# Attention kernel: exponentials three score banks wide instead of two, with a nine-slot ring for P

## The chip, the cores and the metric

The kernel runs on one core of one Trainium2 chip. The time is the device time of one execution in microseconds (us). Every version was run several times; the medians below are of its runs. The kernel before has a median of 1074.17 us in the 15 runs that stand beside the changed one (1072.96 to 1075.71).

A word on names. TensorE (PE in the profile) multiplies matrices, ScalarE (ACT) computes the exponentials, VectorE (DVE) copies and adds, GpSimd (POOL) helps. PSUM is the accumulator memory; the kernel's tile `ps` takes 8 banks of 128 x 512 fp32 in it.

## The reference, cut to what matters

```python
# x: 2048 x 512 bf16, 32 heads of width 16, feed-forward width 1792
qkv = layernorm(x) @ wqkv
scores = einsum("bhqd,bhkd->bhqk", q, k) * 16 ** -0.5      # 32 x 2048 x 2048
o = einsum("bhqk,bhkd->bhqd", softmax(scores), v)
h = x + o @ wo
out = h + relu(layernorm(h) @ w1 + b1) ** 2 @ w2 + b2
```

The scores are 134 million numbers, and each needs one exponential. That is what the kernel is built around.

## The kernel before

Heads are taken in 8 groups of 4, queries in 4 chunks of 512, keys in 16 tiles of 128. One *step* is one key tile for one group and one query chunk: 512 steps. In a step TensorE computes four 128 x 512 score tiles (QK, four matmuls packed into 32 rows each), ScalarE takes their exponential into P, and four packed matmuls multiply P by V (PV). One score tile of 512 columns is called a *unit* here; there are 2048.

```python
        def mk_qk(s):                                   # QK of step s: 4 units
            ...
                for j in range(4):
                    bnk = (4 * s + j) % 6               # score banks 0..5
                    ins = e.matmul(ps[:, bnk, :], lhsT=KT[32 * j:32 * j + 32, g, 128 * t:128 * (t + 1)],
                                   rhs=QT[32 * j:32 * j + 32, slot, :], ..., tile_position=(32 * j, 0))

        def mk_exp(s):                                  # two Exps of 1024 columns each
            for h2 in range(2):
                i = 2 * s + h2
                b0 = (4 * s + 2 * h2) % 6
                u0 = (2 * i) % 8                        # P ring of 8 slots
                n_exp[i] = N("act", 918, ... e.activation(out=PT[:, u0:u0 + 2, :],
                                     in_=ps[:, b0:b0 + 2, :], func=ACTF.Exp) ...,
                    deps=[n_qk[s], n_pv.get(s - 2)], ...)
```

`N(...)` does not issue anything. It hands a task to a list scheduler, which orders the tasks of each engine when the kernel is built, by priority and by its own estimates of when each could start. So a change of one task can move others.

First, everything that is neither score nor output (K and Q projections, V, output projection, feed-forward) goes through bank 7 alone. The evacuation of V alternates between two engines:

```python
            if t % 2 == 0:
                n_e = N("dve", 700, ...)     # VectorE
            else:
                n_e = N("act", 700, ...)     # ScalarE, between Exps
```

Second, where TensorE would idle, the scheduler puts in dummy matmuls by a zero matrix `zw`. They add zero to the output bank, so they are allowed only while an accumulation is open there, and at most six fit one gap:

```python
            if use_dum and e == "pe" and n.crit and self.oacc_open and t - self.free[e] > dum_min_gap:
                k = int((t - self.free[e] - 110.0) // dum_len)
```

Third, the softmax denominators. Each half chunk (four groups) ends with 1/Z, split into two bf16 parts of 16 rows, being spread over 128 partitions by two matmuls per group:

```python
        Rch = sb("Rch", [16, 512], BF16)     # Rcl and bsel likewise 16 rows
        ...
                    e.matmul(ps[:, b, :], lhsT=bsel[:, g4, :, :]..., rhs=Rch[:, :], start=True, stop=False)
                    return e.matmul(ps[:, b, :], lhsT=bsel[:, g4, :, :]..., rhs=Rcl[:, :], start=False, stop=True)
```

## Time and profile before

| what (profiled execution) | before |
|---|---|
| span | 1071.2 us |
| first Exp starts, last Exp ends | 44.6, 1011.2 us |
| busy: TensorE, ScalarE | 92%, 92% |
| mean granted TensorE clock | 0.987 |
| dummy matmuls | 1122 |

The prediction below shows the page and ScalarE's timeline. Two more lines belong here. The first is the page's row of the granted TensorE clock, one digit for each fortieth of the span (9 is 90% and more). The second, from the view of ScalarE's waits, says how long it stood before an Exp in all, how often, and the longest.

```profile
PEclk9996999899999999999999999999999999999999
```

```profile
ACT PT L724 <- PE ps L706: 26.6, 7, 22.1
```

The reader should see 26.6 us of standing, of which one wait is 22.1.

### The profile page before, as it was taken

How to read it: one execution, taken by the hardware profiler on the slowest of the kernel's cores; microseconds unless marked ns; L12 is line 12 of the kernel's file. 1: busy time of each engine (PE TensorE's matmuls, PEld its weight loads, DVE VectorE, ACT ScalarE, POOL GpSimd, SP SyncE). 2: the span in 40 equal slices, each digit the busy share in tenths (PEclk: the TensorE clock that was granted, in tenths of full speed). 3: DMA queues.
4: the chain of work that ended last, by engine and by line, in shares of the span. 5: the costliest groups of instructions: out<-in, count | busy, mean ns of one | idle time of the engine just before them, and what ended most of it. 6: DMA issues, size and time to landing. Idle time of an engine off the chain costs nothing.

```text
span 1071.2 us, 15193 instructions
## 1 busy us (share of the span) xinstructions
PE 980.2 (92%) x6461; PEld 267.0 (25%) x6461; DVE 318.3 (30%) x571; ACT 980.8 (92%) x1086; POOL 195.7 (18%) x312
## 2 busy tenths in 40 slices
PE   3886888999998999999998999999998999999998
PEld 1321222222222222222222222222222222222242
DVE  6504544411134322301145413210054324100151
ACT  6783999899999999999999999999999999999721
POOL 7203433100002411000012401000013400000021
PEclk9996999899999999999999999999999999999999
DMA  4500000000000000000000000000000000000000
GB/s 157 158 1 1 2 1 1 1 2 1 1 2 21 1 11 11 1 2 1 2 5 17 2 13 9 2 1 2 1 11 11 1 16 7 1 1 2 2 1 20
DMA packets 10466, 13.30 MB, mean 12 GB/s; under 512 B 925, under 2 KB 9374, under 8 KB 10398
## 3 DMA queue, kind: packets, MB, share of 16 engines
q1 hardware_dynamic: 8910, 9.71, 2.9%
q0 software_dynamic: 432, 1.57, 0.4%
q8 instruction: 51, 0.84, 0.3%
q10 hardware_dynamic: 1056, 1.05, 0.3%
q14 instruction: 17, 0.14, 0.0%
HBM read 9.97 MB, written 2.10 MB: 11 GB/s over the span
## 4 chain that ended last, share of the span: by engine, by line
ACT 82%; PE 14%; DVE 2%; DMA 1%; issue 1%; SPq 0%; POOL 0%; DVEq 0%
ACT PT L724 81%; PE ps L906 2%; PE ps L406 2%; PE ps L565 2%; PE ps L411 2%; PE ps L933 1%; PE ps L706 1%; DMA b1ld<-in_B_b_dram 1%; PE ps L741 1%; ACT xn L535 1%; PE ps L854 1%; DVE KT L588 1%; PE ps L595 1%; DVE kmx L599 1%; PE ps L660 1%
## 5 line engine op out<-in xcount | busy, mean ns | idle before, releaser
L724 ACT ACTIVATE PT<-ps 128x1024 bf16<-128x1024 f32 x1024 | 940.3, 1248 | 27.1 <-PE ps L706 26.6
L406 PE MATMUL ps<-KT,zw 128*128 128x512 bf16 x1122 | 341.9, 386 | 0.0
L741 PE MATMUL ps<-PT,Vp 128*32 128x512 bf16 x2048 | 205.4, 391 | 16.1 <-ACT PT L724 10.8
L706 PE MATMUL ps<-QT,KT 32*128 32x512 bf16 x2048 | 203.2, 387 | 15.6 <-ACT PT L724 4.5
L628 POOL TENSOR_TENSOR sq<-QT 128x512 bf16<-128x512 bf16 x32 | 33.3, 1039 | 438.8 <-DVE QT L625 424.4
L625 DVE TENSOR_SCALAR QT<-ps,cst 128x512 bf16<-128x512 f32 x32 | 24.0, 751 | 297.6 <-PE ps L565 297.6
L741 PEld LDWEIGHTS ps<-PT,Vp 128*32 128x32 bf16 x2048 | 52.7, 93 | 237.3 <-ACT PT L724 196.4
L706 PEld LDWEIGHTS ps<-QT,KT 32*128 32x128 bf16 x2048 | 51.6, 91 | 213.2 <-ACT PT L724 207.0
L406 PEld LDWEIGHTS ps<-KT,zw 128*128 128x128 bf16 x1122 | 64.9, 97 | 130.6 <-issue 129.6
L752 DVE COPY Osb<-ps 128x512 f32<-128x512 f32 x32 | 22.1, 690 | 141.7 <-PE ps L741 141.7
L924 POOL TENSOR_TENSOR h2T<-t 128x512 bf16<-128x512 bf16 x49 | 50.9, 1039 | 70.2 <-DVE t L921 70.2
L933 PE MATMUL ps<-wbig,h2T 128*128 128x512 bf16 x224 | 59.4, 382 | 1.1 <-issue 0.2
L906 PE MATMUL ps<-hnT,wbig 128*128 128x512 bf16 x224 | 55.6, 380 | 4.0 <-DVE t L921 3.2
L921 DVE TENSOR_SCALAR t<-ps,b1c 128x512 bf16<-128x512 f32 x49 | 36.8, 751 | 62.5 <-PE ps L906 62.5
L592 POOL TENSOR_TENSOR sq<-KT 128x512 bf16<-128x512 bf16 x28 | 29.3, 1047 | 72.8 <-PE ps L595 50.6
L565 PE MATMUL ps<-xnT,Wkp 128*128 128x512 bf16 x128 | 35.9, 407 | 5.3 <-DVE KT L588 2.2
L565 PE MATMUL ps<-xnT,Wqp 128*128 128x512 bf16 x128 | 34.0, 389 | 2.9 <-DVE kmx L599 0.8
L871 POOL TENSOR_SCALAR rstd<-mv 128x1 f32<-128x1 f32 x16 | 3.5, 219 | 165.0 <-DVE mv L869 164.8
L854 PE MATMUL ps<-wo,OT 128*128 128x512 bf16 x128 | 32.6, 381 | 0.9 <-DVE mv L869 0.6
L940 DVE TENSOR_TENSOR ost<-ps,hsb 128x512 bf16<-128x512 f32 x16 | 11.1, 692 | 73.4 <-PE ps L935 73.4
L648 DVE TENSOR_SCALAR qqs<-qqs,qst 128x512 f32<-128x512 f32 x32 | 17.5, 546 | 47.6 <-POOL qst L645 47.6
L588 DVE TENSOR_SCALAR KT<-ps,cst 128x512 bf16<-128x512 f32 x28 | 22.7, 809 | 27.8 <-PE ps L565 27.7
(98 smaller groups left out, 523.4 us busy)
## 6 DMA issues: line engine op xcount, KB each, us to landing
xin<-in_A_x_dram SPq DMA_DIRECT2D x16, 128.0 KB, 2.1
out_dram<-ost SPq DMA_DIRECT2D x16, 128.0 KB, 1.7
wbig<-in_B_w_dram SPq DMA_DIRECT2D x4, 448.0 KB
wbig<-in_B_w_dram SPq DMA_DIRECT2D x1, 1792.0 KB
wbig<-in_A_x_dram ACTq DMA_DIRECT2D x2, 512.0 KB, 9.2
wbig<-in_A_x_dram SPq DMA_DIRECT2D x2, 512.0 KB
h2T<-in_A_wqkv_dram POOLq DMA_DIRECT2D x2, 512.0 KB, 9.0
wv<-in_A_wqkv_dram POOLq DMA_DIRECT2D x1, 512.0 KB, 11.2
```

The source lines that it names most:

```text
L406: return e.matmul(ps[:, OB, :], lhsT=zw[:, :], rhs=KT[:, 0, 0:512], start=False, stop=False, skip_group_check=True)
L565: ins = e.matmul(ps[:, b, :], lhsT=W[:, dt, 4 * g:4 * g + 4, :].rearrange("p j r -> p (j r)"), rhs=xnT[:, dt, tok0:tok0 + 512], start=(dt ...
L588: n_e = N("dve", 660, (lambda g, kc: lambda e, b: e.tensor_scalar(out=KT[:, g, 512 * kc:512 * (kc + 1)], in0=ps[:, b, :], scalar1=cst[:, 1 ...
L628: n_s = N("pool", 1050, lambda e, b: e.tensor_tensor(out=sq[:, sslot, :], in0=QT[:, slot, :], in1=QT[:, slot, :], op=ALU.mult), deps=[n_e, ...
L706: ins = e.matmul(ps[:, bnk, :], lhsT=KT[32 * j:32 * j + 32, g, 128 * t:128 * (t + 1)], rhs=QT[32 * j:32 * j + 32, slot, :], start=True, st ...
L724: n_exp[i] = N("act", 918, (lambda b0, u0: lambda e, b: e.activation(out=PT[:, u0:u0 + 2, :], in_=ps[:, b0:b0 + 2, :], func=ACTF.Exp))(b0, ...
L741: ins = e.matmul(ps[32 * j:32 * j + 32, OB, :], lhsT=bass.AP(vb.tensor, vb.offset, [[vb.ap[0][0], 128], [1, 32]]), rhs=PT[:, u, :], start= ...
L854: mms = [(lambda g, i: lambda e, b: e.matmul(ps[:, b, :], lhsT=OT[:, g, 128 * i:128 * (i + 1)], rhs=wo[:, g, :], start=(g == 0), stop=(g = ...
L906: ins = e.matmul(ps[:, b, :], lhsT=w1[:, dt, 128 * ft:128 * (ft + 1)], rhs=hnT[:, dt, :], start=(dt == 0), stop=(dt == DT - 1))
L921: n_r = N("dve", 680, (lambda ft, slot: lambda e, b: e.tensor_scalar(out=t1[:, slot, :], in0=ps[:, b, :], scalar1=b1c[:, ft:ft + 1], scala ...
L924: n_s = N("pool", 1050, (lambda ft, slot: lambda e, b: e.tensor_tensor(out=h2T[:, ft, :], in0=t1[:, slot, :], in1=t1[:, slot, :], op=ALU.m ...
L933: mms = [(lambda ft, i: lambda e, b: e.matmul(ps[:, b, :], lhsT=h2T[:, ft, 128 * i:128 * (i + 1)], rhs=w2[:, ft, :], start=(ft == 0), stop ...
```

## The change

The intent: fewer and wider Exps, in the hope that a part of an Exp's time does not grow with its width. Units are taken in threes across step boundaries. QK becomes a task of three matmuls into banks 0 to 2 or 3 to 5, the Exp reads three banks at once, and P becomes a ring of nine slots. PV still takes four units, so it now reads from two Exps.

```diff
-        PT = sb("PT", [128, 8, 512], BF16)
+        PT = sb("PT", [128, 9, 512], BF16)
 ...
-        def mk_qk(s): ...
-        def mk_exp(s): ...
+        UPI = 3
+        NU = 4 * NSTEP
+        NI = (NU + UPI - 1) // UPI
+        PTR = 9
+        def mk_qkexp(i):
+            us = [u for u in range(UPI * i, min(UPI * i + UPI, NU))]
+            deps = [n_exp.get(i - 2)]
 ...
+                    bnk = 3 * (i % 2) + k
 ...
+            n = N("pe", 330, fn, deps=deps, crit=1, name="qk%d" % i, prio=3 * i, order=[n_qk.get(i - 1)],
+                  slack=cfg.get("slack_qk", 600.0))
 ...
+            b0 = 3 * (i % 2)
+            u0 = (UPI * i) % PTR
+            pvd = (UPI * i + nu - 1 - PTR) // 4
+            n_exp[i] = N("act", 64 + 427 * nu, ... out=PT[:, u0:u0 + nu, :], in_=ps[:, b0:b0 + nu, :] ...,
+                deps=[n, n_pv.get(pvd) if pvd >= 0 else None], ..., prio=3 * i + 1, ...)
 ...
-            deps = [n_exp[2 * s + 1]]
+            deps = [n_exp[(4 * s + 3) // UPI]]                      # PV
-            n = N("pe", 330, fn, ..., prio=2 * s + 1, order=[n_pv.get(s - 1), n_qk.get(s)],
+            n = N("pe", 330, fn, ..., prio=4 * s + 3, order=[n_pv.get(s - 1)],
 ... (priorities of the other parts rescaled to match; ones_row replaced by onesb)
```

## The prediction

> **What bounds the kernel now.** I read the page first: busy shares, then the chain that ended last, then the costliest groups. TensorE and ScalarE tie at 92%, so the shares alone do not name the bound.

> ```profile
> PE 980.2 (92%) x6461; PEld 267.0 (25%) x6461; DVE 318.3 (30%) x571; ACT 980.8 (92%) x1086; POOL 195.7 (18%) x312
> ...
> ACT 82%; PE 14%; DVE 2%; DMA 1%; issue 1%; SPq 0%; POOL 0%; DVEq 0%
> ...
> L724 ACT ACTIVATE PT<-ps 128x1024 bf16<-128x1024 f32 x1024 | 940.3, 1248 | 27.1 <-PE ps L706 26.6
> L406 PE MATMUL ps<-KT,zw 128*128 128x512 bf16 x1122 | 341.9, 386 | 0.0
> ```

> The second line (shares of the chain that ended last) decides: 82% of the chain is ScalarE, nearly all of it the Exp of line 724. TensorE's 92% is partly padding: line 406 is a dummy matmul by a zero matrix, put in to keep the clock up, 1122 times. So ScalarE sets the pace from the first Exp (44.6 us) to the last (about 1011 us). What lies before and behind, some 105 us, the change does not touch in substance.

> Next I asked the timeline for ScalarE alone, to see whether those 966 us are one unbroken row.

> ```profile
> 48.84 25.90 ACT L724 ACTIVATE PT<-ps 128x1024 bf16<-128x1024 f32 x28
> 74.33 0.90 ACT L670 ACTIVATE Vp<-ps 128x512 bf16<-128x512 f32 x1
> 97.30 92.00 ACT L724 ACTIVATE PT<-ps 128x1024 bf16<-128x1024 f32 x100 [22.07 <-PE ps L706]
> 189.53 12.94 ACT L724 ACTIVATE PT<-ps 128x1024 bf16<-128x1024 f32 x14 [0.23 <-PE ps L706]
> 202.74 1.94 ACT L724 ACTIVATE PT<-ps 128x1024 bf16<-128x1024 f32 x2 [0.28 <-PE ps L706]
> 205.21 1.94 ACT L724 ACTIVATE PT<-ps 128x1024 bf16<-128x1024 f32 x2 [0.54 <-PE ps L706]
> 207.76 1.94 ACT L724 ACTIVATE PT<-ps 128x1024 bf16<-128x1024 f32 x2 [0.61 <-PE ps L706]
> 210.79 800.39 ACT L724 ACTIVATE PT<-ps 128x1024 bf16<-128x1024 f32 x872 [1.09 <-PE ps L706]
> ```

> Two things stand out. From 210.79 on, 872 Exps run without a gap: (800.39 - 1.305) / 871 = 0.9174 us from one to the next (1.305 is the median record of one, from the view of line 724). And there is one hole of 22.07 us before 97.30. It follows exactly one small instruction, the last evacuation of V (line 670 at 74.33), which stands behind the first 32 Exps. The full timeline shows what happens in the hole.

> ```profile
> 74.33 0.90 ACT L670 ACTIVATE Vp<-ps 128x512 bf16<-128x512 f32 x1
> ...
> 75.61 1.04 PE L565 MATMUL ps<-xnT,Wkp 128*128 128x512 bf16 x4
> ...
> 87.68 1.89 PE L565 MATMUL ps<-xnT,Wkp 128*128 128x512 bf16 x4 [0.85 <-DVE QT L625]
> ```

> The K preparation of head group 1 starts only at 75.61. It has one PSUM bank to go through (bank 7; banks 0 to 5 hold scores, bank 6 the output), and the V tile held that bank until ScalarE emptied it. So the whole chain of K and Q for group 1 runs bare, and the TensorE clock drops on the way (1.89 us for four matmuls in place of 1.04; the view by stretches has a granted clock of 0.50 from 84 to 96).

> [...]

> **The change, part by part.**

> *Wider Exps.* 2048 units of 512 columns in pairs were 1024 instructions; in threes they are 682 of 1536 columns and one of 1024. Cost before: 1024 x 0.9174 = 939.4 us. [...]

> *The hole.* The diff does not mention it. But the order of instructions in the two built kernels does: before, ScalarE has 4 Exps, an evacuation of V, 28 Exps, the last evacuation of V; after, it has 1 Exp, an evacuation, 2 Exps, the last evacuation, then 679 Exps in a row. Bank 7 comes free after the third Exp. On TensorE the K projections of group 1 now stand between QK units from the first few on, and its K maxima and Q projection are done by about the 14th unit, where group 1 is first needed by unit 21. So I expect the 22.1 us to be gone.

> *The start.* I followed the first ten Exps by hand, with durations from the trace (0.97 us for four projection matmuls to the next instruction, 0.8 for the K evacuation, 0.7 for V, 0.6 for V on ScalarE). The fourth V tile cannot be computed until the K tile before it has left bank 7, and the fourth Exp now stands behind its evacuation: Exp 3 comes out about 2.3 us late, and some tenths follow. Cost 2.5 us.

> *Slack at the score banks.* Before, QK for a step waits for an Exp's end and has one Exp of 0.917 us to be ready; it starts some 0.07 us after the end of that record (500.01 us in the timeline) and takes 0.39. An Exp that must not be late has to begin about 0.1 us before its predecessor's end (isolated records are 1.02 long against 0.917), so roughly 0.3 us is spare. After, the window is 1.344 us and QK is no longer than before: about 0.75 us spare, or 0.44 where a PV of 0.33 goes first.

> *Slack at the P ring.* Nine slots of which three are written: an Exp now needs a PV whose input came, in one of four cases, from the Exp two before it. That PV has 1.344 us where it had two Exps of 0.917. In the built order PV stands ahead of QK there, so QK remains the later of the two and the ring does not set the pace.

> *TensorE.* The same 2048 QK and 2048 PV matmuls; dummies fall from 1122 to 840. Three packed matmuls cost nearly what four did (some 0.30 to 0.33 us to the next instruction), so per 12 units 4 x 0.30 + 3 x 0.33 = 2.2 us of 5.38 is bound up; 3.2 us remain for three filler chains of 0.97. Still not the bound.

> Sum: 1073.9 - 21.8 - 22.1 + 2.5 = 1032.5 us. I add 1.5 us for late QKs where projection or feed-forward chains stand in front (0.97 us against 0.44 spare, and the builder may put one up to 0.6 us into the way), and get **1034 us**, a ratio of 0.963.

> **The rivals.** (a) *Only the instruction count counts*: the hole stays or moves to another group, since K preparation of later groups has 21 slots of 1.344 us, 28.7 us in all, to pass one bank. Then 1073.9 - 21.8 = 1052, just at 2%. For it speaks that bank 7 is still alone; against it that before, groups 2 to 7 were prepared in 29.3 us each with no hole at all. (b) *TensorE becomes the bound in the first quarter*: with fewer dummies (in the K phases nearly none), the clock falls to half, and four projection matmuls of 1.89 us no longer fit a slot. Before has such a stretch: from 200 to 211 the granted clock is 0.53 and ScalarE lost 2.5 us in four gaps. If each of the seven groups had one, that would be 7 x 2.5 = 17.5 us, thus about 1050. Against it: before had phases just as thin around 100, 118, 137 and 173 us (2.7 to 2.8 of 4 us busy) at full clock. (c) *The fixed cost is not fixed*: [...]gain 21.8 would shrink to nothing and only the hole would be won: also near 1052. [...]

> **Range and chances.** The lower end is the sum without the start's stall and without the cold stretch of before: 1073.9 - 21.8 - 22.1 - 2.5 = 1027.5. The upper end takes in a good part of (b), 1047. Faster by over 2% means under 1052.4; only (a), (c) or a full (b) would miss that, together about 8%. A slowdown would need TensorE to set the pace throughout: 1%.

> **What would show it.** In the changed profile's ScalarE timeline: long unbroken rows at 1.344 us an Exp (wider: (c) or a slack that is too small); no gap over 5 us near 75 us; a gap of 2 to 3 us within the first five Exps. The Exp group should be busy about 918 us, idle before it under 10. The granted clock in the first 230 us should be above 0.9; if below, with short gaps "<-PE ps" at the QK line, (b) is at work. I am wrong if the K preparation leaves a hole elsewhere, or if waits for PV (the P ring) show up before the Exps.

The forecast's sum came to 1034 us: 1073.9 - 21.8 (wider Exps) - 22.1 (the hole) + 2.5 (the start) + 1.5 (late QKs). Measured since are 1.3434 us for a wide Exp and 21.5 us less for all Exps together.

## The result and the profile after

| | before | after |
|---|---|---|
| median of the runs | 1074.17 us (15 runs) | 1047.05 us (9 runs) |
| lowest to highest | 1072.96 to 1075.71 | 1044.13 to 1055.36 |
| ratio | | 0.9762 (95%: 0.9742 to 0.9781), faster |
| span of the profiled execution | 1071.2 | 1050.0 |
| mean granted clock in it | 0.987 | 0.966 |
| dummy matmuls | 1122 | 840 |

Ratios are the mean time of one kernel's runs over that of the other's runs of the same rounds, so not quite the ratio of the medians quoted. The predicted direction came true, but the median is 13 us above the predicted 1034 and 0.05 us above the upper end of the range. The spread of the runs also grew from under 3 us to 11, and it goes with the clock: of ten executions of this one kernel the quickest (1044.13 us) had a mean granted clock of 0.977 and the slowest (1055.36) one of 0.961, with the others in order between them. The profiled execution took 1051.96 us at 0.966, so it is one of the slower ones.

The page of the changed kernel, first busy shares, then the clock row, the shares of the chain that ended last, and the groups of the Exps and of the dummies:

```profile
PE 958.6 (91%) x6179; PEld 273.8 (26%) x6179; DVE 322.4 (31%) x570; ACT 965.6 (92%) x745; POOL 197.2 (19%) x312
...
PEclk9999999999989998999989998999889998989999
...
ACT 64%; PE 27%; DVE 5%; DMA 1%; issue 1%; POOL 1%; SPq 0%
...
L735 ACT ACTIVATE PT<-ps 128x1536 bf16<-128x1536 f32 (+1 forms) x683 | 925.1, 1568 | 20.3 <-PE ps L715 18.5
L405 PE MATMUL ps<-KT,zw 128*128 128x512 bf16 x840 | 256.0, 397 | 0.0
```

The line of ScalarE's waits before the Exps:

```profile
ACT PT L735 <- PE ps L715: 18.5, 36, 1.8
```

Three readings. The number of Exps fell as planned (683). The chain's share on TensorE went up from 14% to 27%. And the waits before the Exps have changed their kind: before it was one wait of 22 us, now it is 36 waits of at most 1.8 us. The clock row has gone from two dips to many, all after the first quarter.

ScalarE's timeline (start, duration, engine, line, what, how many, and in brackets the idle time before with what ended it) shows both sides of it:

```profile
44.92 1.45 ACT L735 ACTIVATE PT<-ps 128x1536 bf16<-128x1536 f32 x1 [1.78 <-PE ps L715]
46.27 0.59 ACT L668 ACTIVATE Vp<-ps 128x512 bf16<-128x512 f32 x1
46.74 2.80 ACT L735 ACTIVATE PT<-ps 128x1536 bf16<-128x1536 f32 x2
50.15 0.60 ACT L668 ACTIVATE Vp<-ps 128x512 bf16<-128x512 f32 x1 [0.60 <-PE ps L658]
50.64 39.51 ACT L735 ACTIVATE PT<-ps 128x1536 bf16<-128x1536 f32 x29
...
294.93 2.79 ACT L735 ACTIVATE PT<-ps 128x1536 bf16<-128x1536 f32 x2 [0.48 <-PE ps L715]
298.27 1.45 ACT L735 ACTIVATE PT<-ps 128x1536 bf16<-128x1536 f32 x1 [0.54 <-PE ps L715]
301.17 1.45 ACT L735 ACTIVATE PT<-ps 128x1536 bf16<-128x1536 f32 x1 [1.46 <-PE ps L715]
...
422.92 72.65 ACT L735 ACTIVATE PT<-ps 128x1536 bf16<-128x1536 f32 x54 [0.29 <-PE ps L715]
```

The last evacuation of V (line 668) now stands behind three Exps, and no hole follows. The row from 422.92 gives the new cadence: (72.65 - 1.45) / 53 = 1.3434 us, where 1.45 is the duration of an isolated record. The prediction had 1.344. Around 295 to 302, however, Exps come late one after another. The view by stretches (busy time of PE, PEld, DVE, ACT and POOL with the number of instructions, then the granted clock) names what is special there:

```profile
285.00:289.00 4.00, 3.84 (x28) 0.94 (x27) 3.94 (x6) 4.00 (x5) 0.00 (x0) 1.00 0.01 4
289.00:302.00 13.00, 12.49 (x59) 2.96 (x59) 4.03 (x6) 10.52 (x9) 0.00 (x0) 0.61 0.00 0
```

The clock is at half for most of these 13 us, and TensorE is busy nearly throughout: it has become the bound there.

**Where the time went.** From each trace I took the end of every Exp and compared it with the end of the one before plus the ideal cadence (0.917 us for two banks, 1.344 for three). What is over is lateness; I sorted it by whether it lies in or next to a half-clock stretch. All in us:

| | before | after | difference |
|---|---|---|---|
| first Exp starts at | 44.6 | 44.9 | +0.3 |
| Exps at the ideal cadence | 939.0 | 917.5 | -21.5 |
| the hole near 75 us | 22.7 | 0 | -22.7 |
| late in or next to other half-clock stretches | 3.0 | 17.5 | +14.5 |
| late elsewhere | 1.8 | 9.9 | +8.1 |
| from the last Exp to the end | 60.0 | 60.0 | 0 |
| span | 1071.2 | 1050.0 | -21.2 |

(The parts add up to the spans within rounding.) The predicted gains came in full. Then 22.6 us were given back in two ways, of which the prediction had allowed 4.0 (2.5 for the start and 1.5 for late QKs).

**What precedes a half-clock stretch.** In the changed kernel there are twelve of them before the tail, each 3.41, 6.83 or 10.24 us long in the trace's records of the granted clock (four, seven and one of them), that is, one to three times 3.41 us. Seven begin at the 1/Z broadcasts, the other five at changes of head group. Here is the timeline of TensorE at one broadcast (289.7) and at one group change (930.9):

```profile
289.74 0.38 PE L791 MATMUL ps<-Rch,bsel 16*128 16x512 bf16 x1 [0.24 <-DVE Rcl L783]
289.97 0.37 PE L793 MATMUL ps<-Rcl,bsel 16*128 16x512 bf16 x1
...
291.12 0.38 PE L791 MATMUL ps<-Rch,bsel 16*128 16x512 bf16 x1
291.35 0.37 PE L793 MATMUL ps<-Rcl,bsel 16*128 16x512 bf16 x1
291.80 0.62 PE L752 MATMUL ps<-PT,Vp 128*32 128x512 bf16 x4
```

```profile
931.18 0.39 PE L715 MATMUL ps<-QT,KT 32*128 32x512 bf16 x3
...
932.20 0.39 PE L715 MATMUL ps<-QT,KT 32*128 32x512 bf16 x3 [0.62 <-ACT PT L735]
...
933.54 0.62 PE L752 MATMUL ps<-PT,Vp 128*32 128x512 bf16 x4 [0.95 <-ACT PT L735]
...
934.63 1.03 PE L405 MATMUL ps<-KT,zw 128*128 128x512 bf16 x2
```

**What makes Exps late elsewhere.** Exp j needs QK j, and QK j needs the banks of Exp j-2. Reading each late Exp of the changed kernel at full clock, I found one rule: if QK starts t us after the end of Exp j-2, the Exp is late by about t - 0.80 (1.33, 1.21 and 0.95 us gave 0.53, 0.41 and 0.15). A PV takes 0.33 us and stands ahead of QK. A chain of four projection or feed-forward matmuls takes up to 0.97, so together they overrun.

### The profile page after: what moved, and what is told of

Same layout as the page of the kernel before. It is cut to its first block, busy times and chain, and to the rows that moved or that the text cites. A ratio compares the mean times of both kernels' runs of the same rounds, so it can differ in the third digit from the quotient of the medians.

```text
span 1050.0 us, 14273 instructions
## 1 busy us (share of the span) xinstructions
PE 958.6 (91%) x6179; PEld 273.8 (26%) x6179; DVE 322.4 (31%) x570; ACT 965.6 (92%) x745; POOL 197.2 (19%) x312
## 4 chain that ended last, share of the span: by engine, by line
ACT 64%; PE 27%; DVE 5%; DMA 1%; issue 1%; POOL 1%; SPq 0%
ACT PT L735 63%; PE ps L715 5%; PE ps L752 4%; PE ps L946 4%; PE ps L405 3%; PE ps L563 3%; PE ps L867 2%; PE ps L919 2%; PE ps L410 2%; DVE kmx L597 2%; DVE KT L586 1%; DMA b1ld<-in_B_b_dram 1%; PE ps L593 1%; PE ps L658 1%; ACT xn L533 1%
## 5 line engine op out<-in xcount | busy, mean ns | idle before, releaser
L735 ACT ACTIVATE PT<-ps 128x1536 bf16<-128x1536 f32 (+1 forms) x683 | 925.1, 1568 | 20.3 <-PE ps L715 18.5
L715 PE MATMUL ps<-QT,KT 32*128 32x512 bf16 x2048 | 275.0, 396 | 10.8 <-ACT PT L735 4.5
L405 PE MATMUL ps<-KT,zw 128*128 128x512 bf16 x840 | 256.0, 397 | 0.0
L752 PE MATMUL ps<-PT,Vp 128*32 128x512 bf16 x2048 | 210.9, 403 | 28.3 <-ACT PT L735 14.1
L715 PEld LDWEIGHTS ps<-QT,KT 32*128 32x128 bf16 x2048 | 66.8, 91 | 205.0 <-issue 131.2
L626 POOL TENSOR_TENSOR sq<-QT 128x512 bf16<-128x512 bf16 x32 | 33.5, 1046 | 428.1 <-DVE QT L623 425.3
L405 PEld LDWEIGHTS ps<-KT,zw 128*128 128x128 bf16 x840 | 56.1, 98 | 107.3 <-issue 90.8
L763 DVE COPY Osb<-ps 128x512 f32<-128x512 f32 x32 | 22.1, 689 | 105.7 <-PE ps L752 105.6
L867 PE MATMUL ps<-wo,OT 128*128 128x512 bf16 x128 | 35.6, 408 | 1.0 <-DVE qqs L632 0.7
L563 PE MATMUL ps<-xnT,Wkp 128*128 128x512 bf16 x128 | 33.1, 381 | 3.0 <-DVE KT L586 1.9
L586 DVE TENSOR_SCALAR KT<-ps,cst 128x512 bf16<-128x512 f32 x28 | 22.6, 808 | 28.3 <-PE ps L563 28.3
L796 DVE TENSOR_TENSOR OT<-Osb,ps 128x512 bf16<-128x512 f32 x32 | 21.7, 687 | 27.6 <-PE ps L793 27.0
```

Source lines behind the costliest of these rows:

```text
L405: return e.matmul(ps[:, OB, :], lhsT=zw[:, :], rhs=KT[:, 0, 0:512], start=False, stop=False, skip_group_check=True)
L563: ins = e.matmul(ps[:, b, :], lhsT=W[:, dt, 4 * g:4 * g + 4, :].rearrange("p j r -> p (j r)"), rhs=xnT[:, dt, tok0:tok0 + 512], start=(dt ...
L586: n_e = N("dve", 660, (lambda g, kc: lambda e, b: e.tensor_scalar(out=KT[:, g, 512 * kc:512 * (kc + 1)], in0=ps[:, b, :], scalar1=cst[:, 1 ...
L626: n_s = N("pool", 1050, lambda e, b: e.tensor_tensor(out=sq[:, sslot, :], in0=QT[:, slot, :], in1=QT[:, slot, :], op=ALU.mult), deps=[n_e, ...
L735: n_exp[i] = N("act", 64 + 427 * nu, (lambda b0, u0, nu: lambda e, b: e.activation(out=PT[:, u0:u0 + nu, :], in_=ps[:, b0:b0 + nu, :], fun ...
L752: ins = e.matmul(ps[32 * j:32 * j + 32, OB, :], lhsT=bass.AP(vb.tensor, vb.offset, [[vb.ap[0][0], 128], [1, 32]]), rhs=PT[:, u, :], start= ...
```

## The experiments

Twelve kernels ran, all correct. They came in four batches; each has its own runs of the kernel before (medians 1074.64, 1074.04, 1073.5 and 1073.67 us). The changed kernel itself was not run again beside them, so a difference of 1 or 2 us against its 1047.05 says nothing.

**My theory** after the result: (1) the hole's end was a side effect of the new order, and the width alone gives 21.5 us, of which most is given back; (2) the half-clock stretches come from too little of the array in use, in the broadcasts by 16 rows and in the group changes by missing dummies; (3) the rest is the deadline just told. **Rivals:** that busy time drives the clock, so rows make no difference; that the P ring is what makes Exps late.

### Run 1: the kernel before, with only the last V tile moved to VectorE

```diff
-            if t % 2 == 0:
+            if t % 2 == 0 or t == 15:
```

> The kernel before, with one edit: the last V tile is evacuated by VectorE in place of ScalarE, so bank 7 comes free early; Exps stay 1024 columns wide. Theory (the hole is a separate gain, independent of the width): the 22.07 us hole before group 1 is gone, 1074.2 - 22.1 = 1052 us, within 3 us; 1024 Exps still at 0.917 us. Rival (the hole only moves, since one bank serves all K preparation): a new gap of 5 us or more at a later group change, time 1060 us or above.

Measured: 1051.57 us (1050.03 to 1053.43, 4 runs), ratio 0.9783. The verdict by the 2% mark is unclear; the size is as expected. ScalarE's timeline of this run has no hole:

```profile
48.62 0.64 ACT L670 ACTIVATE Vp<-ps 128x512 bf16<-128x512 f32 x1
49.26 13.12 ACT L724 ACTIVATE PT<-ps 128x1024 bf16<-128x1024 f32 x14
...
64.92 36.94 ACT L724 ACTIVATE PT<-ps 128x1024 bf16<-128x1024 f32 x40 [0.45 <-PE ps L706]
```

What follows: one condition in the old kernel yields 23.1 us (1074.64 - 1051.57). The whole change with its wider Exps, at 1047.05, is only 4.5 us better than that by the medians (some 2 us by the ratios, whose intervals overlap), where its width alone should give 21.5. This shows the hole's share; where the other 17 us or more went is for the next runs.

### Run 2: the changed kernel, with full-array fillers at the group changes

Three zero matmuls go into the QK's own bank ahead of it, so that no open accumulation is needed.

```diff
+                for _ in range(3 if (i - 2) % 64 == 0 and i > 2 else 0):
+                    e.matmul(ps[:, 3 * (i % 2), :], lhsT=zw[:, :], rhs=KT[:, 0, 0:512], start=True, stop=True, ...)
```

> The changed kernel with three full-array zero matmuls ahead of the QK unit that falls into the dummy-free stretch at every third group change (10 places). In the changed kernel's trace the five half-clock windows that start at 226.8, 404.3, 493.0, 755.9 and 933.3 us lie there and cost some 4.6 us of late Exps. Theory (thin use of the array in one 3.4 us window drops the clock): those five are gone, the ones in the 1/Z broadcast stay; about 1042 us. Rival (the drops are chance, or follow from something else than thin TensorE use): as many drops as before, 1047 us.

Measured: 1046.95 us (1045.16 to 1048.96), ratio 0.9746. In the trace the five half-clock stretches at group changes are gone and the seven at broadcasts are still there, with one at 77.5 us. Lateness at half clock fell from 17.5 to 10.8 us in the profiled executions. Yet the median did not move against 1047.05, which is a miss in time. The clocks of its four runs lie between 0.974 and 0.979, and the changed kernel had 0.974 in its median run. So the profiled execution of the changed kernel, one of its slower ones, makes the fillers look better than they are.

### Run 3: the changed kernel, with the broadcasts on 128 rows

The added rows are zeros. Nothing else in the instruction order differs.

```diff
-        Rch = sb("Rch", [16, 512], BF16)      # Rcl, bsel likewise
+        Rch = sb("Rch", [128, 512], BF16)
...
+            e.memset(Rch[:, :], 0.0)
+            e.memset(Rcl[:, :], 0.0)
```

> The changed kernel with the 1/Z broadcast matmuls over 128 rows in place of 16 (112 rows of zeros): same number, same length and same order of instructions. Theory (what counts is the share of the array in use, rows times columns times time): the half-clock windows at the broadcasts (182.4, 291.6, 414.5, 530.6, 650.0, 766.1, 885.6 us in the changed kernel) vanish, those at group changes stay; about 1038 us. Rival (what counts is whether TensorE is busy at all): nothing changes, 1047 us, as TensorE is busy just as long.

Measured: 1037.06 us (1035.37 to 1038.37), ratio 0.9647. Ten us gained by multiplying by zeros. The timeline at the same place shows the broadcasts at the same duration and the PV after them at full speed, and the view by stretches (second fence) has full clock:

```profile
290.90 0.39 PE L793 MATMUL ps<-Rch,bsel 128*128 128x512 bf16 x1 [0.25 <-DVE Rcl L785]
291.12 0.38 PE L795 MATMUL ps<-Rcl,bsel 128*128 128x512 bf16 x1
...
292.94 0.40 PE L754 MATMUL ps<-PT,Vp 128*32 128x512 bf16 x4
```

```profile
285.00:300.00 15.00, 13.88 (x93) 3.63 (x90) 8.28 (x12) 15.00 (x12) 0.62 (x3) 1.00 0.00 1
```

All seven drops at broadcasts are gone; three stretches remain (170.8, 553.1 and 921.7 us). The rival that busy time is what counts is refuted: windows at the broadcasts of this run kept the clock though matmuls occupied only 0.51 of them, and in the changed kernel windows occupied for 0.52 to 0.67 lost it. The other half of the expectation failed: of the five stretches at group changes only the last stayed, though nothing was edited there. The traces suggest why. In each of them all stretches start on one grid of 3.41 us, and the grid lies differently from trace to trace. Wherever the window is laid, the lowest share around four of these changes (223.8, 401.8, 490.1 and 753.1 us in the changed kernel) is 0.33 in both traces; in the windows of the grid it was 0.35 to 0.38 in the changed kernel and 0.38 to 0.43 here. So a part of the ten us could be the grid's luck. Runs 4 and 2, which both have the fillers and no stretch at a group change, differ by the rows alone: 10.9 us. Lateness at half clock is 3.0 us; lateness elsewhere is unchanged at 9.9, so the two costs are separate.

### Run 4: both

> Both edits of the two runs before in one kernel. Theory: no or hardly any half-clock window between the first and the last Exp, granted clock above 0.99, about 1034 us. The rest of the miss against 1027.5 us is then some 8 us of Exps late behind filler chains at full clock. Rival (late Exps come from the filler order or the P ring and the clock is a by-product): 1044 us or more with the clock at 1.0.

The edit is that of runs 2 and 3 together. Measured: 1036.07 us (1034.88 to 1037.13), ratio 0.9638; one stretch is left (170.4 us), with 2.0 us of lateness, and 11.0 elsewhere. The fillers add no clear gain on top of the rows. Against run 2, in the same rounds, the rows are worth 10.9 us (1046.95 - 1036.07; ratios 0.9746 and 0.9638).

### Run 5: a ring of twelve slots

```diff
-        PTR = 9
+        PTR = 12
```

(To make room, the residual's input buffer went from four slots to two, and the bias row shares a tile.) With nine slots, Exp i overwrites units up to 3i - 7, so it needs PV (3i - 7)//4, whose own input is Exp i-2 in three of four cases. With twelve slots that is Exp i-3 or i-4.

> The changed kernel with a P ring of twelve slots in place of nine (room made by a two-slot input buffer of the epilogue and by putting the b2 row on a free partition). Theory (QK is the later of the two, the ring does not set the pace): within 4 us of the changed kernel, 1043 to 1051 us. Rival (the tighter ring holds the Exps up): 1040 us or less.

Measured: 1045.85 us (1045.26 to 1047.04), ratio 0.9741. No clear gain; lateness elsewhere is 9.3. Here PV stands ahead of QK in the built order, so QK remains the later of the two.

### Run 6: the changed kernel with the last V tile moved

The edit is that of run 1.

> The changed kernel with the last V tile evacuated by VectorE, the edit that took the hole out of the kernel before. Theory: only the start gains, where Exp 1 and Exp 3 came 0.5 and 1.2 us late: about 1045 us, and no other gap opens. Rival (more hole was left than seen): 1040 us or less.

Measured: 1047.42 us (1046.81 to 1048.62), ratio 0.9754; no gain, a small miss. Lateness elsewhere is 8.8.

### Run 7: QK ahead of PV

```diff
-            n = N("pe", 330, fn, ..., name="qk%d" % i, prio=3 * i, ...
+            n = N("pe", 330, fn, ..., name="qk%d" % i, prio=3 * i - 7, ...
```

> The changed kernel with one priority changed, so that the QK of a unit stands ahead of the PV that becomes ready at the same moment. Theory (QK has to start within about 0.8 us of the Exp's end, and a PV of 0.33 us, or 0.55 at half clock, in front of it eats the slack): late Exps outside half-clock windows fall from some 10 us to 3, those inside roughly by half, 1034 to 1038 us; the half-clock windows stay. Rival (the filler chains alone make QK late): 1044 us or more. A second rival: PV is then late for the ring, seen as Exps that wait for PV.

Measured: 1050.12 us (1046.16 to 1050.75), ratio 0.977. This is a clear miss. The waits of ScalarE say why:

```profile
ACT PT L735 <- PE ps L752: 16.9, 31, 1.3
ACT PT L735 <- PE ps L715: 1.8, 1, 1.8
```

Line 752 is PV. The Exps now wait for the ring instead of the banks, just as long. So my theory (3) was incomplete: QK and PV have the *same* deadline, 0.80 us after the end of Exp j-2, one for the banks and one for the ring. In this trace the rule of t - 0.80 holds for the PV (starts of 1.32, 1.20 and 0.94 us gave 0.54, 0.42 and 0.15). Whichever goes second misses it. The second rival came true.

### Run 8: runs 2, 3, 6 and 7 together

> All edits together: full-row broadcast, zero matmuls at every third group change, last V tile on VectorE, QK ahead of PV. Theory: little is left but the Exps themselves: first Exp at 44.7, 682 at 1.3433 us and one at 0.917, 60 us of tail: 1025 to 1029 us, and late Exps in sum under 4 us.

Measured: 1035.79 us (1035.7 to 1036.88), ratio 0.9646. The expectation was missed by 7 us: it is no better than run 4, with lateness elsewhere at 10.3 and the Exps waiting for PV (5.4 us in 14 waits).

### Run 9: ring of twelve and QK first, on the changed kernel

> The changed kernel with both the ring of twelve and QK ahead of PV; each alone gave nothing. Theory (QK and PV form a pair of which the later one has to start within 0.8 us of the Exp's end: QK for the banks, PV for the nine-slot ring, in three of four units and not in one of four as the prediction had it; only with both edits is one of the two free): late Exps outside half-clock windows fall from 9 us to 4 or less, in those windows to half or less; 1034 us, and 1038 at most. The half-clock windows themselves stay at about ten. Rival (filler chains in front of either make everything late): 1044 us or more.

The edit is that of runs 5 and 7. Measured: 1062.8 us (1061.87 to 1065.32), ratio 0.99: a miss by 25 us, in the wrong direction. ScalarE's timeline:

```profile
72.72 0.79 ACT L668 ACTIVATE Vp<-ps 128x512 bf16<-128x512 f32 x1
96.69 4.24 ACT L735 ACTIVATE PT<-ps 128x1536 bf16<-128x1536 f32 x3 [23.18 <-PE ps L715]
```

The hole is back: the new priorities have put the last evacuation of V behind 21 Exps again. Apart from the hole, lateness at half clock is 10.3 and elsewhere only 4.0, where the changed kernel has 9.9. So the theory could still be right; the run alone cannot say.

### Run 10: everything

Runs 2, 3, 5, 6 and 7 together.

> The same with the full-row broadcast, the zero matmuls at every third group change and the last V tile on VectorE. Theory: late Exps in sum under 5 us, almost no half-clock window, 1027 to 1030 us, below all runs so far. Rival: no better than 1035.8 us, the best so far.

Measured: **1029.21 us** (1027.34 to 1031.49), ratio 0.9578, the best. Lateness elsewhere is 3.9, at half clock 2.8; the sum of 6.7 is above the 5 expected. The line of ScalarE's waits, and one row of its timeline:

```profile
ACT PT L739 <- PE ps L719: 5.7, 11, 1.8
```

```profile
151.11 629.18 ACT L739 ACTIVATE PT<-ps 128x1536 bf16<-128x1536 f32 x468 [0.63 <-PE ps L719]
```

468 Exps in a row without an idle record between them, at (629.18 - 1.45) / 467 = 1.3442 us.

### Run 11: the kernel before, with V moved and broadcasts on 128 rows

> The kernel before (pairs of banks) with the last V tile on VectorE and the full-row broadcast: the two repairs that it can take as well. Theory: its one half-clock stretch at a broadcast (180.6 us, some 4 us of late Exps) goes: 1048 us. Against the run with all edits this leaves the width of the Exps: [...]18 to 21 us between the two. Rival (wide Exps are worth little even when nothing holds them up): under 12 us between them.

Measured: 1047.93 us (1047.8 to 1050.68), ratio 0.9764. This is the old width with both of its faults cured. Against run 10, which stands in the same rounds, it is 18.7 us slower. That is what three banks are worth once the rest is in order: 21.5 less the lateness that the wide form still has more of (3.9 + 2.8 against 1.4 + 2.2 us) would be 18.4.

### Run 12: run 9 with the last V tile moved

The edit is run 9's with run 1's line on top. (The text below calls run 9 "the run before last but one".)

> The kernel of the run before last but one (twelve slots and QK ahead of PV, on the changed kernel) with the last V tile evacuated on VectorE, without full rows and without fillers. That run had taken 1062.8 us, and its trace shows why: the hole was back (23.2 us with no Exp, after a V evacuation on ScalarE at 72.7 us that the new order had put behind 21 Exps), while the Exps late outside the hole and outside half-clock stretches had fallen from 9.9 us in the changed kernel to 4.0. My theory, that QK and PV share one deadline and both have to be freed: the hole goes (-23), the 4.0 us stay, the half-clock stretches stay (11 to 17 us): 1037 to 1043 us, some 5 us under the changed kernel with only the V tile moved (1047.4). Rival: the order of QK and PV is worth nothing even with both free (each alone moved nothing): 1046 to 1048 us.

Measured: 1040.06 us (1037.88 to 1041.54, 5 runs), ratio 0.9678. No hole; lateness elsewhere is 3.4 us, at half clock 13.0. Against run 6, which lacks only the ring and the order, that is 7.4 us better in time and 5.4 us less lateness elsewhere. Ring alone, order alone: no clear gain. Both: seven. The shared deadline is shown, and the rival (the order is worth nothing) is refuted.

The lateness of the versions on one sheet (profiled executions, us):

| | median | hole | at half clock | elsewhere |
|---|---|---|---|---|
| before | 1074.17 | 22.7 | 3.0 | 1.8 |
| run 1: before + V | 1051.57 | 0 | 4.6 | 1.7 |
| run 11: before + V + rows | 1047.93 | 0 | 2.2 | 1.4 |
| after | 1047.05 | 0 | 17.5 | 9.9 |
| run 2: after + fillers | 1046.95 | 0 | 10.8 | 10.5 |
| run 3: after + rows | 1037.06 | 0 | 3.0 | 9.9 |
| run 12: after + V + ring + order | 1040.06 | 0 | 13.0 | 3.4 |
| run 10: all | 1029.21 | 0 | 2.8 | 3.9 |

**What stays open.** A profile is one execution, and the half-clock column moves from one execution to the next, so it does not carry differences of a few us; the runs with their rounds do. That the rows in use count is shown at the broadcasts (seven drops with 16 rows, none with 128 in run 3). For the rest it is a count that fits 88 drops; the exact limit is not known, since about a dozen windows at 0.36 to 0.38 kept the clock. Run 2's fillers removed five stretches from the profiled execution and no time that the runs could show; how much of that is their own cost on TensorE was not measured.

## Why the prediction was right or wrong, point by point

*Wider Exps, 21.8 us.* Right. The cadence is 1.3434 us against a predicted 1.344, and the ideal sum fell by 21.5. Rival (c), a fixed cost that grows with width, is refuted by that: had that cost grown in step with the width, a wide Exp would take one and a half times 0.9174, or 1.376 us.

*The hole, 22.1 us.* Right, in size (22.7 with its neighbours) and in cause. Run 1 produces it by one line without the change, and run 9 loses it again through the built order.

*The start, 2.5 us.* Right in place, too large: Exp 1 came 0.5 us late and Exp 3 1.2, together 1.7. The gap of 2 to 3 us that should have shown it did not appear; the widest between two of the first five Exps is 1.10.

*"Slack at the P ring": one of four cases, the ring does not set the pace.* The count was wrong: it is three of four, as worked out at run 5. The conclusion held for the kernel as built, since PV stood ahead of QK (one wait for PV, 0.3 us in all), but run 7 shows that the ring has no slack to give. The prediction looked at the banks and the ring one at a time; they are one deadline for two tasks.

*"I add 1.5 us for late QKs."* The mechanism was right and the size was off. The spare time of 0.44 us beside a PV was close (0.80 - 0.33 = 0.47 by the rule from the trace). The term was mis-sized by the count: 1.5 us is about three full overruns of 0.97 - 0.44 = 0.53, and the trace has about 45 late Exps at full clock, of 0.2 us on average. Lateness elsewhere rose by 8.1 us in all, start included, against 4.0 for both terms.

*"TensorE: still not the bound", and rival (b).* This is the step that failed, and the largest. The prediction counted busy time and reasoned that phases as thin as before had kept their clock. It named the drop of the clock as a rival, but set it in the K phases of the first quarter and priced it there. In truth that quarter had only two half-clock stretches, of 3.4 us each (182.4 and 226.8 us), neither from the K work, and the drops went on to the end, at the broadcasts and group changes. They cost 14.5 us more than before in the profiled execution, and less in the median run, which was 4.9 us faster (1047.05 against 1051.96). The clue was in the kernel before: its stretch from 200 to 211 us, which the prediction cites, begins at its first 1/Z broadcast, where busy time was 0.48 of the window but only 0.25 of the array was in use. The prediction took it for a thin phase like the others. What changed at the others can be counted in the two kept traces, from 1 us before the first to 1 us after the last broadcast of each half chunk. Before, that first one has 2 dummies, the next six have 7 each, and the lowest share in a window there was 0.25 against 0.40 to 0.47. After, all seven have 0 or 2 dummies, and the share in the window ahead of the drop is 0.24 to 0.33. So what had happened at one broadcast happened at all seven. Putting dummies back there was not tried; putting rows there was: run 3, whose instruction order is the same, takes 1037.06 us, 3 us above the forecast.

*The observables.* "Busy about 918, idle under 10" was wrong (925.1 and 20.3), and it pointed the right way: short gaps before the Exps at the QK line, which the prediction had named as the sign of (b). "The clock in the first 230 us above 0.9" came true and misled, because the trouble lies after it.

*The 3.41 us, and what counts in them.* In each trace the stretches are multiples of 3.41 us on one grid, and the grid's place against the first instruction differs (the first grid line lies 1.51 us after it in the changed kernel's trace, 0.12 in run 3's). That could also explain why one and the same kernel had clocks from 0.961 to 0.977, but no run tests that. Busy time did not separate the drops: windows with 0.51 of it kept the clock in run 3, and windows with 0.52 to 0.67 lost it in the changed kernel. Nor does one long idle time stand ahead of them. In the 3.41 us ahead of the drop in the old hole (81.1 us) the longest idle time of TensorE is 1.00 us, and the share in use was 0.35; ahead of the seven drops at the broadcasts of the changed kernel the longest is 0.40 us.

## What to carry to other kernels

When a change makes one engine's work fewer and larger, ask what the padding on the other engine had been doing, and look in the old trace for the one place where its clock already falls: that was the place where the new kernel fell often. Here matmuls with 16 rows could be given 112 rows of zeros at no cost in duration that the trace shows (0.37 to 0.39 us each, before and after), and that was worth some ten us. When two tasks share a deadline, freeing one of them shows nothing; free both, and check in the built order that nothing else has moved.
